# Linear attention with soft mixture of experts on one core: who copies the output banks, and a wait of three engines in front of the last branch

## Chip, core and metric

The kernel runs on one core of a Trainium2 chip. The metric is the device time of one execution in microseconds (us). Engines: PE (TensorE), DVE (VectorE), ACT (ScalarE), POOL (GpSimd) and SP (SyncE, here the queue that issues nearly all DMAs). All of a core's DMAs are carried by 16 DMA engines.

## What is computed

A gated linear attention over 4 batches x 8 heads, 768 steps, head size 48, whose result is the input x (3072 x 384) of a soft mixture of 8 experts with 4 slots each:

```python
f = 1 / (1 + np.exp(-f_logit))
for t in range(S):
    state = f[:, :, t, :, None] * state + np.einsum('bhd,bhe->bhde', k[:, :, t], v[:, :, t])
    y[:, :, t] = np.einsum('bhd,bhde->bhe', q[:, :, t], state)
x = y.transpose(0, 2, 1, 3).reshape(B * S, H * D)

logits = x @ phi                                  # 3072 x 32
d = softmax(logits, axis=0); c = softmax(logits, axis=1)
slot_input = d.T @ x                              # 32 x 384
slot_out[e] = np.maximum(slot_input[e] @ w1[e], 0) @ w2[e]
out = c @ slot_out                                # 3072 x 384
```

The output is 4.7 MB. The last line is where the change lies: 3072 x 32 by 32 x 384.

## The kernel before

Sixteen pairs of heads run through the attention in about 117 us, with loads on SP all the way. Then come the mixture's slots, the experts' first weights (`up`, L615) and second weights (`down`, L664), and the output.

The output columns are cut into three **parts** of 128 columns (`PARTS`, L32). For each part: PE multiplies the experts' second weights (`down`), DVE scales the result (`slots_out`, L675), PE sums it over the experts' rows (`slots_sum`, L678), ACT copies that to `s4` (`slots_copy`, L682), and PE forms the output rows from `s4` and the mixing weights `cT` (`combine`, L705). The rows come in six chunks of 128 for each batch: four "main" ones, and two "shared" ones whose mixing weights share a transposed tile. `combine` therefore runs twice for a part: main (four PSUM banks of 512 columns: 4 batches x 128) and shared (two banks).

**PSUM units.** PSUM is handed out by the planner as three large units of kind `a` (1024 columns, two banks) and two small ones of kind `b` (512 columns, one bank); see L232 and `unit` (L235). Before the change, main takes two `a` units and shared takes one, both of its banks in that unit. The small units carry, among others, the results of `down` (`po`) and of `slots_sum` (`so`).

**Copies and stores.** Each bank is copied to SBUF by one instruction of 512 columns (`out_copy`, L714): even banks by ACT, odd banks by DVE (L989), so each unit is read by both engines. All copies have the line of the helper, L321. The stores (`store`, L717) go out on SP: two banks together (512 KB) in parts 0 and 1, one bank (256 KB) in part 2, except that bank 4 of part 2, the first shared one, is issued on ACT's own DMA queue (L994). In part 2 the order on SP is 0, 1, 2, 3, 5.

**Order.** A planner (`Plan.run`, L119) orders everything: every operation has a cost on its engine, what it reads, writes and takes, and a due time; the planner always starts the operation that can start first. `ENDING` (L35) sets the due times of the last phase as a written sequence: `d0` a quarter of a `down` half in part 0, `s0` its sum, `c0` its two combines, and so on. Its end is `... d2 c1 s2 c2 c2`: the shared combine of part 1, the sum of part 2, and the two combines of part 2. The planned order is emitted at L1003 to L1019; `last_of` keeps the last instruction of each operation that isn't on SP, for the weights' loads that are paced by it.

**The branch.** The fast path is right only if no gate is extreme. A flag (`flag_1` to `flag_3`) says so, is loaded into a register `bad` of the engines at L1005, and after all stores have been emitted, every engine meets `tc.If(bad > 0)` (L1078). The block behind it, `general()`, is the slow path, some thousands of instructions; it is jumped over when the flag is 0, as it is for these inputs. What follows it is the end of the program: SP waits for the landings of the stores, and all engines meet in a barrier (listed under L1078 and L1133).

Of the kernel before, what the change touches and what calls it, by code (L numbers as in the profile page):

```python
# [34 lines left out]
ENDING = (  # L35
    "d0 d0 d0 d0 d0 d0 d0 d0 d1 d1 s0 d1 c0 d1 d1 d1 d1 d1 c0 s1 d2 d2 c1 d2 d2 d2 d2 d2 d2 c1 s2 c2 c2"
).split()

SWAP = NM // 2

# [32 lines left out]
class Plan:  # L73
# [22 lines left out]
    def op(self, name, engs, fn, *args, r=(), w=(), x=(), due=0.0, take=(), free=(), kb=0, home=False, ni=0):  # L96

        name, mode = name if isinstance(name, tuple) else (name, None)
        deps = set()
        for key in r:  # L100
            if key in self.writer:
                deps.add(self.writer[key])
        for key in (*w, *x):
            if key in self.writer:
                deps.add(self.writer[key])
            deps.update(self.readers.get(key, ()))
        fixed = self.fixed and "SP" not in engs
        o = Op(len(self.ops), name, engs, fn, args, due, deps, take, free, kb, home, ni, mode, fixed)
        self.ops.append(o)
        for key in w:  # L110
            self.writer[key] = o
            self.readers[key] = []
        for key in r:
            self.readers.setdefault(key, []).append(o)
        for key in (*r, *w):
            self.uses.setdefault(key, []).append(o)
        return o
# [96 lines left out]
def gla_soft_moe_kernel(ctx: ExitStack, tc: tile.TileContext, q, k, f, v, vt, phi, w1, w2, out):  # L214
# [7 lines left out]
    nc = tc.nc  # L222
# [3 lines left out]
    def P(shape, name, dt=F32):  # L226
        return pool.tile(shape, dt, tag=name, name=name)
# [5 lines left out]
    un = {}  # L233

    def unit(key):  # L235
        u = plan.unit_of[key]
        un[key] = ps.tile([128, 1024 if u[0] == "a" else 512], F32, tag=u, name=str(key[0]), bufs=1)
        return un[key]
# [9 lines left out]
    kb = [P([128, S], f"kb{i}") for i in range(N_K)]  # L248
# [71 lines left out]
    def copy(o, dst, src):  # L320
        {"ACT": nc.scalar.copy, "DVE": nc.vector.tensor_copy, "POOL": nc.gpsimd.tensor_copy}[o.eng](dst, src)  # L321
# [248 lines left out]
    def piece(part, kk):  # L570

        n = 8 * WIDE * part + WIDE * kk
        return n // PIECE, n % PIECE
# [128 lines left out]
    def staged(part, x, n=1):  # L702
        return w1b[4 + part][:, 4 * WIDE * x : 4 * WIDE * (x + n)]

    def combine(o, part, shared):  # L705

        v = [u[:, 512 * k : 512 * k + 512] for u in [unit(("pf", part, x)) for x in ((2,) if shared else (0, 1))] for k in range(2)]
        n = 128 // len(v)
        for b in range(B):
            for x, u in enumerate(v):  # L710
                gs = slice(n * x, n * x + n)
                nc.tensor.matmul(u[:, WIDE * b : WIDE * b + WIDE], cT[gs, b, shared], s4[gs, PARTS[part]], start=b == 0, stop=True, skip_group_check=True)  # L712

    def out_copy(o, part, x):  # L714
        copy(o, staged(part, x), un["pf", part, x // 2][:, 512 * (x % 2) : 512 * (x % 2) + 512])

    def store(o, part, x, n):  # L717
        at = 4 * WIDE * (6 * part + x)
# [3 lines left out]
    op = plan.op  # L722
# [181 lines left out]
    n, asked = 0, set()  # L904
# [17 lines left out]
    y = (NP - 1) * T  # L922
# [30 lines left out]
    for j in range(2):  # L953
        for hf in range(2):
            key, d = ("up", j, hf), z + 5 + 4 * j + hf
# [3 lines left out]
            key = ("turn", j, hf)  # L959
# [3 lines left out]
    def at(kind, part, n=0):  # L963

        return z + 100 + 0.1 * [x for x, name in enumerate(ENDING) if name == kind + str(part)][n]
# [5 lines left out]
    for part in range(len(PARTS)):  # L971
        key = ("po", part)
        for j in range(2):
            for k0 in range(0, 8, 2):
                ws = sorted({("w2", 2 * qq + j, piece(part, kk)[0]) for qq in range(4) for kk in (k0, k0 + 1)})
                take = [(key, "b")] if (j, k0) == (0, 0) else []
                op(("down", "strips"), {"PE": 0.47}, down, part, j, k0, k0 + 2, r=[("hT", j, k0 // 4), *ws], w=[key], due=at("d", part, 4 * j + k0 // 2), take=take, ni=32)
        op("so1", {"DVE": 0.4}, slots_out, part, r=[key, "rz", ("pin1", 0), "psi"], w=[("sob", part)], due=at("d", part, 7) + 0.05, free=[key])
        op(("so2", "square"), {"PE": 0.25}, slots_sum, part, r=[("sob", part), "same"], w=[("so", part)], due=at("s", part), take=[(("so", part), "b")], ni=4)
        op("so3", {"ACT": 0.32}, slots_copy, part, r=[("so", part)], w=[("s4", part)], due=at("s", part) + 0.05, free=[("so", part)])  # L980
        for shared in range(2):
            keys, d = [("pf", part, x) for x in ((2,) if shared else (0, 1))], at("c", part, shared)
            op(
                ("comb", "pf" + str(shared)), {"PE": 0.9}, combine, part, shared, r=[("s4", part), *(("cT", b) for b in range(B))], w=keys, due=d,
                take=[(key, "a") for key in keys], ni=16 * len(keys),
            )
            for x in range(4 * shared, 4 + 2 * shared):
                key, late = ("pf", part, x // 2), (part, x) == (2, 4)
                op("oute", [{"ACT": 0.59}, {"DVE": 0.69}][x % 2], out_copy, part, x, r=[key, ("upw", 1, 0), ("upw", 1, 1)], w=[("st", part, x)], due=d + 0.05 + 0.001 * x, free=[key])  # L989

                n = 1 if part == 2 else 2
                if (x + 1) % n == 0:
                    x0 = x + 1 - n
                    op("store", {"ACT" if late else "SP": 0.45}, store, part, x0, n, r=[("st", part, y) for y in range(x0, x0 + n)], due=d + 0.06, kb=256 * n)  # L994
    plan.fixed = False

    def emit(o):
        o.fn(o, *o.args)

    order = plan.run(dict(PE=2.3, POOL=2.3, DVE=2.0, ACT=2.1, SP=0.4))  # L1000
    written = nc.cur_bb.bb.instructions
    last_of, steps = {}, []
    for o in order:  # L1003
        if o.name == "so2" and o.args == (1,):
            bad = nc.values_load(gbad[:1, :1], min_val=0, max_val=1)  # L1005
        n0 = len(list(written))
        emit(o)
        new = list(nc.cur_bb.bb.instructions)[n0:]
        if o.name in ("lw1", "lw2"):

            before = [(d.end, n, d) for n, d in enumerate(steps) if d.end < o.begin - plan.LAT]
            if before:
                tc.add_manual_dep(
                    new[-1], last_of[max(before)[2].n], mybir.DependencyInfo(mybir.DependencyClass.Sync, mybir.DependencyReason.DATA),
                    reason="pace",
                )
        elif o.eng != "SP":
            steps.append(o)
            last_of[o.n] = new[-1].name  # L1019
    to_psi = ("gmax", "lte", "gexp", "te", "ele", "pi", "pie", "tm", "tmt", "tm2", "tmb", "twb", "twb2", "twd", "psi")  # L1020
    ending = [o for o in order if o.n >= tail_from and o.name not in (*to_psi, "flag1", "flag2", "flag3")]
    resident = [o for o in order if o.name == "lw1" and o.n < tail_from]
# [115 lines left out]
```

## Time and profile before

| | |
|---|---|
| time, median of 3 runs | 168.49 us (167.91 to 168.71) |
| the profiled execution | 168.29 us |
| its span, first to last instruction | 166.6 us |
| PE busy | 153.7 us, 92% of the span |
| DVE, ACT, POOL busy | 116.6, 94.2, 89.9 us |
| output stores | 6 of 512 KB and 5 of 256 KB on SP, 1 of 256 KB on ACT |
| issue to landing, median | 3.5 us (512 KB), 3.9 us (256 KB on SP), 4.1 us (ACT) |

The span runs from the first to the last instruction; 1.69 us of the execution lie outside it. Engines with a `q` behind the name (SPq, ACTq, PEldq) are the engines' instruction queues: DMA issues, branches and semaphore waits are listed there, and they do not count as busy time. `out<-in` names tiles: `w1a<-pf` is a copy from a combine's PSUM unit to its place in SBUF, `out_dram<-w1a` is a store. A DMA counts as landed when all of the 16 engines that carry it have reported. The DMA queues are q1 (SP's), q10 (ACT's), and q8 and q14, which load the engines' instructions.

### The profile page before, as it was taken

What the parts mean: (1) busy time and instruction counts of PE and PEld (TensorE: products, weight loads), DVE (VectorE), ACT (ScalarE), POOL (GpSimd) and SP (SyncE); (2) the same over time, 40 slices, a digit from 0 to 9 for tenths busy, and PEclk for the clock granted to TensorE, in tenths of its full rate; (3) what the DMA queues carried; (4) which work ended last, traced back from release to release, by engine and by line L of the source; (5) the groups of instructions that cost most, each with busy time, mean ns of one, the idle gap of its engine ahead of it and who ended that gap; (6) DMA issues with size and microseconds to landing.
All of it is one profiled execution on the core that took longest, in us unless ns stands there. A gap on an engine that the chain in (4) does not pass through costs nothing.

```text
span 166.6 us, 6386 instructions
## 1 busy us (share of the span) xinstructions
PE 153.7 (92%) x2724; PEld 123.3 (74%) x2724; DVE 116.6 (70%) x167; ACT 94.2 (57%) x166; POOL 89.9 (54%) x87
## 2 busy tenths in 40 slices
PE   5999999999999999999998999999899999999800
PEld 2367879889998969889896889988655449788700
DVE  4899999989979876898996989838432216043330
ACT  5899597967977949678783872631521121232310
POOL 5108969889889886897997889660000001000000
PEclk9999999999999999999999999999999999999985
DMA  5999999999999999999997559999999792055784
GB/s 134 320 407 370 390 399 398 399 398 393 395 393 397 397 397 399 396 398 398 398 377 248 182 173 293 340 363 407 398 398 389 233 360 85 6 215 211 281 295 151
DMA packets 20609, 54.05 MB, mean 325 GB/s; under 512 B 2288, under 2 KB 2912, under 8 KB 20576
## 3 DMA queue, kind: packets, MB, share of 16 engines
q1 hardware_dynamic: 20432, 53.34, 86.2%
q8 instruction: 22, 0.36, 0.9%
q10 hardware_dynamic: 144, 0.26, 0.4%
q14 instruction: 11, 0.09, 0.1%
HBM read 48.87 MB, written 4.72 MB: 322 GB/s over the span
## 4 chain that ended last, share of the span: by engine, by line
PE 67%; DVE 14%; POOL 5%; issue 4%; DMA 3%; ACT 3%; SPq 1%; POOLq 0%; ACTq 0%; DVEq 0%
PE sc L379 10%; PE y L404 9%; PE po L670 7%; PE up L625 7%; PE y L427 6%; PE kv L413 5%; PE kt L367 5%; DVE Lb L338 5%; PE xt L438 4%; PE pl L459 3%; PE pf L712 3%; DMA kb<-in_k_dram 3%; DVE scb L384 3%; POOL ce L545 2%; PE pi L502 2%
## 5 line engine op out<-in xcount | busy, mean ns | idle before, releaser
L347 POOL TENSOR_TENSOR kb<-kb,gb 112x768 f32<-112x768 f32 x15 | 27.4, 1830 | 16.3 <-ACT gb L341 12.8
L338 DVE TENSOR_TENSOR_SCAN Lb<-starts,fb 112x768 f32<-112x768 f32 (+1 forms) x17 | 35.1, 2063 | 1.6 <-ACT fb L334 1.6
L384 DVE TENSOR_TENSOR scb<-sc,mask 128x768 f32<-128x768 f32 x32 | 29.2, 950 | 4.0 <-PE sc L379 3.9
L321 POOL COPY pbx<-pb 112x240 f32<-112x240 f32 x16 | 26.6, 1663 | 4.6 <-ACT pb L344 4.6
L379 PE MATMUL sc<-qb,kb 48*128 48x128 f32 x384 | 26.5, 282 | 0.5 <-DVE kta L321 0.4
L404 PE MATMUL y<-scb,va 128*48 128x128 f32 (+1 forms) x384 | 25.9, 276 | 0.0
L379 PEld LDWEIGHTS sc<-qb,kb 48*128 48x128 f32 x384 | 22.9, 187 | 3.4 <-DVE kta L321 0.6
L321 ACT COPY yT<-y 112x768 f32<-112x768 f32 x16 | 12.8, 798 | 19.6 <-PE y L427 19.6
L347 POOL TENSOR_TENSOR qb<-qb,pb 112x768 f32<-112x768 f32 x13 | 23.7, 1827 | 0.0
L404 PEld LDWEIGHTS y<-scb,va 128*48 128x48 f32 (+1 forms) x384 | 21.9, 130 | 0.8 <-DVE scb L384 0.4
L545 POOL TENSOR_TENSOR ce<-ce,cm 128x256 f32<-128x256 f32 x4 | 4.6, 1156 | 29.7 <-DVE cm L542 29.3
L321 DVE COPY kta<-kt 128x672 f32<-128x672 f32 x14 | 11.8, 846 | 7.6 <-PE kt L367 7.6
L341 ACT ACTIVATE gb<-Lb 112x768 f32<-112x768 f32 (+1 forms) x17 | 13.7, 805 | 4.9 <-DVE Lb L338 4.9
L334 ACT ACTIVATE fb<-fb,one 112x768 f32<-112x768 f32 (+1 forms) x17 | 15.2, 897 | 0.6
L330 ACT ACTIVATE fb<-fb 112x768 f32<-112x768 f32 (+1 forms) x17 | 13.7, 805 | 2.7 <-DMA fb<-in_f_dram 2.7
L427 PE MATMUL y<-qb,sb 48*48 48x128 f32 x320 | 14.6, 285 | 0.0
L413 PE MATMUL kv<-va,kta 128*64 128x48 f32 (+1 forms) x384 | 14.4, 220 | 0.0
L413 PEld LDWEIGHTS kv<-va,kta 128*64 128x64 f32 (+1 forms) x384 | 12.4, 130 | 2.6 <-ACT kta L321 0.8
L344 ACT ACTIVATE pb<-Lb 112x768 f32<-112x768 f32 (+1 forms) x17 | 13.5, 792 | 0.0
L427 PEld LDWEIGHTS y<-qb,sb 48*48 48x48 f32 x320 | 11.1, 162 | 2.7 <-DVE sb L417 2.4
L367 PE MATMUL kt<-ident,kb 112*128 112x112 f32 x96 | 12.7, 266 | 0.2 <-POOL kb L347 0.2
L321 DVE COPY w1a<-pf 128x512 f32<-128x512 f32 x9 | 5.8, 687 | 9.5 <-ACT w1a L321 9.5
(154 smaller groups left out, 276.9 us busy)
## 6 DMA issues: line engine op xcount, KB each, us to landing
w1a<-in_w_dram SPq DMA_DIRECT2D x34, 384.0 KB, 7.6
kb<-in_k_dram SPq DMA_DIRECT2D x16, 384.0 KB, 7.4
fb<-in_f_dram SPq DMA_DIRECT2D x15, 384.0 KB, 7.3
qb<-in_q_dram SPq DMA_DIRECT2D x15, 384.0 KB, 7.3
va<-in_v_dram SPq DMA_DIRECT2D x16, 288.0 KB, 7.3
out_dram<-w1a SPq DMA_DIRECT2D x6, 512.0 KB, 3.5
scb<-in_w_dram SPq DMA_DIRECT2D x4, 384.0 KB, 6.9
out_dram<-w1a SPq DMA_DIRECT2D x5, 256.0 KB, 3.9
```

Source lines behind the costliest of these rows:

```text
L321: {"ACT": nc.scalar.copy, "DVE": nc.vector.tensor_copy, "POOL": nc.gpsimd.tensor_copy}[o.eng](dst, src)
L330: nc.scalar.activation(t, t, AF.Exp, scale=-1.0, accum_out=esum[:, n : n + 1])
L334: nc.scalar.activation(t, t, AF.Ln, bias=one[:PW])
L338: nc.vector.tensor_tensor_scan(Lb[i % N_L][:PW, cs], flat(starts)[:PW, cs], fb[i % N_F][:PW, cs], 0.0, op0=ALU.mult, op1=ALU.add)
L341: nc.scalar.activation(gb[i % N_G][:PW, cs], Lb[i % N_L][:PW, cs], AF.Exp)
L347: (nc.vector if o.eng == "DVE" else nc.gpsimd).tensor_tensor(t, t, by, op=ALU.mult)
L367: nc.tensor.transpose(u[:, C * m : C * m + PW], kb[i % N_K][:PW, C * m : C * m + C], ident[:PW, :PW])
L379: nc.tensor.matmul(u[:, 512 * r + C * m : 512 * r + C * m + C], kb[i % N_K][rs, cs], qb[i % N_Q][rs, cs], start=True, stop=True,)
L384: nc.vector.tensor_tensor(scb[i % N_SC][:, :, h], un["sc", i, h].rearrange("p (r x) -> p r x", r=2)[:, :, : 3 * C].rearrange("p r (m t) -> ...
L404: nc.tensor.matmul(u[rows(at), y_cols(m)], va[:, v0 : v0 + (D if at else 64)], scb[i % N_SC][:, r, h, m % 3], start=m % 3 == 0, stop=False ...
L413: nc.tensor.matmul(u[rows(r), :, m], ktb[i % N_KT][:, m, rows(r)], vb[i % N_V][:, m, r], start=True, stop=True)
L427: nc.tensor.matmul(u[at : at + D, y_cols(m)], sb[i % N_S][rs, :, m - 1], qb[i % N_Q][rs, C * m : C * m + C], start=False, stop=m in (2, 5) ...
```

## The change

1. **Copies.** In the main combine each unit (two banks) is read by one engine: unit 0 by ACT, unit 1 by DVE. In parts 0 and 1 that is one instruction of 1024 columns, in part 2 two of 512 each. The shared combine takes two units, one bank in each: bank 4 is copied by ACT, bank 5 by DVE. These two units are of kind `a` in parts 0 and 1, and of kind `b` in part 2.
2. **Stores.** The same pieces go out on the same queues; in part 2 the order on SP becomes 0, 2, 1, 3, 5.
3. **The wait.** After all has been emitted, and in front of the branch, PE, DVE and POOL each get a `nop` that waits until the third last store in the planner's order (`HELD = -3`) has landed. ACT and SP get none.

```diff
+HELD = -3
...
-        v = [u[:, 512 * k : 512 * k + 512] for u in [unit(("pf", part, x)) for x in ((2,) if shared else (0, 1))] for k in range(2)]
+        if shared:
+            v = [unit(("pf", part, x))[:, :512] for x in (2, 3)]
+        else:
+            v = [u[:, 512 * k : 512 * k + 512] for u in [unit(("pf", part, x)) for x in (0, 1)] for k in range(2)]
...
-    def out_copy(o, part, x):
-        copy(o, staged(part, x), un["pf", part, x // 2][:, 512 * (x % 2) : 512 * (x % 2) + 512])
+    def out_copy(o, part, x, n):
+        key, at = (("pf", part, x // 2), 512 * (x % 2)) if x < 4 else (("pf", part, x - 2), 0)
+        copy(o, staged(part, x, n), un[key][:, at : at + 512 * n])
...
-            keys, d = [("pf", part, x) for x in ((2,) if shared else (0, 1))], at("c", part, shared)
+            keys, d = [("pf", part, x) for x in ((2, 3) if shared else (0, 1))], at("c", part, shared)
+            kind = "b" if shared and part == 2 else "a"
             op(
                 ("comb", "pf" + str(shared)), {"PE": 0.9}, combine, part, shared, r=[("s4", part), *(("cT", b) for b in range(B))], w=keys, due=d,
-                take=[(key, "a") for key in keys], ni=16 * len(keys),
+                take=[(key, kind) for key in keys], ni=16 * (1 if shared else 2) * 2,
             )
-            for x in range(4 * shared, 4 + 2 * shared):
-                key, late = ("pf", part, x // 2), (part, x) == (2, 4)
-                op("oute", [{"ACT": 0.59}, {"DVE": 0.69}][x % 2], out_copy, part, x, r=[key, ("upw", 1, 0), ("upw", 1, 1)], w=[("st", part, x)], due=d + 0.05 + 0.001 * x, free=[key])
-
-                n = 1 if part == 2 else 2
-                if (x + 1) % n == 0:
-                    x0 = x + 1 - n
-                    op("store", {"ACT" if late else "SP": 0.45}, store, part, x0, n, r=[("st", part, y) for y in range(x0, x0 + n)], due=d + 0.06, kb=256 * n)
+
+            for key, eng in zip(keys, ("ACT", "DVE")):
+                x0, n = (2 + key[2], 1) if shared else (2 * key[2], 2)
+                step = 1 if part == 2 else n
+                for x in range(x0, x0 + n, step):
+                    op(
+                        "oute", {eng: {"ACT": 0.14, "DVE": 0.07}[eng] + {"ACT": 0.45, "DVE": 0.61}[eng] * step}, out_copy, part, x, step,
+                        r=[key, ("upw", 1, 0), ("upw", 1, 1)], w=[("st", part, y) for y in range(x, x + step)], due=d + 0.05 + 0.001 * x, free=[key],
+                    )
+
+            n = 1 if part == 2 else 2
+            for x in (4, 5)[::n] if shared else (0, 2, 1, 3) if n == 1 else (0, 2):
+                late = (part, x) == (2, 4)
+                op("store", {"ACT" if late else "SP": 0.45}, store, part, x, n, r=[("st", part, y) for y in range(x, x + n)], due=d + 0.06, kb=256 * n)
...
+        elif o.name == "store":
+            last_of[o.n] = new[-1].name
         elif o.eng != "SP":
...
+    stored = last_of[[o for o in order if o.name == "store"][HELD].n]
+    for eng in (nc.tensor, nc.vector, nc.gpsimd):
+        eng.nop()
+        tc.add_manual_dep(
+            list(written)[-1], stored, mybir.DependencyInfo(mybir.DependencyClass.Sync, mybir.DependencyReason.DATA), reason="leave",
+        )
```

## The prediction

> **What bounds the kernel now.** The change touches only what follows the last down products, so I first read the chain that ended last for its final pieces, then the windows of the last 10 us, then the rows of the stores and of the branch. The page's span, PE's last products from the timeline (start, duration; both combines of part 2), and the end of the chain (start, duration):
>
> ```profile
> span 166.6 us, 6386 instructions
> ...
> 156.15 2.27 PE L712 MATMUL pf<-pin,cT 32*128 32x128 f32 x48 [0.43 <-ACT pin L321]
> ...
> 157.36 0.59 ACT w1a L321
> ...
> 157.98 0.52 DVE w1a L321
> ...
> 158.59 0.59 DVE w1a L321
> ...
> 159.18 0.68 DVE w1a L321
> ```
>
> Computation ends at 159.18 + 0.68 = 159.86; the span ends at 166.6. So 6.7 us are stores and closing. The columns of the next view are busy time by engine, then granted clock, share of the 16 DMA engines, GB/s:
>
> ```profile
> 158.80:160.20 1.40, 0.00 (x0) 0.00 (x0) 1.06 (x2) 0.25 (x1) 0.00 (x0) 1.00 0.99 360
> 160.40:161.10 0.70, 0.00 (x0) 0.00 (x0) 0.00 (x0) 0.00 (x0) 0.00 (x0) 1.00 0.15 47
> 161.20:164.00 2.80, 0.00 (x0) 0.00 (x0) 0.00 (x0) 0.00 (x0) 0.00 (x0) 0.50 1.01 372
> 164.20:164.50 0.30, 0.00 (x0) 0.00 (x0) 0.00 (x0) 0.00 (x0) 0.00 (x0) 0.50 0.12 48
> 164.70:166.60 1.90, 0.00 (x0) 0.00 (x0) 0.00 (x0) 0.00 (x0) 0.00 (x0) 0.50 0.00 0
> ```
>
> The stores move at 360 to 372 GB/s, with a hole from about 160.4 to 161.1 (share 0.15), and after 164.1 two engines of sixteen (0.12) work on alone until 164.7.  Why the hole? The issues on the two queues (start, duration):
>
> ```profile
> 157.97 0.33 SPq L719 DMA_DIRECT2D out_dram<-w1a  x1
> 158.70 0.33 SPq L719 DMA_DIRECT2D out_dram<-w1a  x1
> 159.08 1.61 ACTq L719 DMA_DIRECT2D out_dram<-w1a  x1
> 159.12 1.70 SPq L719 DMA_DIRECT2D out_dram<-w1a  x1
> 161.39 0.69 SPq L719 DMA_DIRECT2D out_dram<-w1a  x1
> DMA to landing us min/median/max: 3.7/3.7/3.7
> ```
>
> A store takes 0.33 us to issue, but those of 159.1 take 1.6 and 1.7. The last one (its landing is the last row) goes out at 161.39 and lands at 165.1, though its data was ready at 159.86. Beside the stall lie the branch and its code pages:
>
> ```profile
> L1078 POOLq COMPARE_BRANCH  x1: 65/65/65, 141.4 to 141.4; - x1
> L1078 PEldq COMPARE_BRANCH  x1: 491/491/491, 157.3 to 157.3; - x1
> L1078 PEldq EVENT_SEMAPHORE  x1: 51/51/51, 158.5 to 158.5; - x1
> L1078 DVEq COMPARE_BRANCH  x1: 84/84/84, 159.1 to 159.1; - x1
> L1078 ACTq COMPARE_BRANCH  x1: 68/68/68, 160.7 to 160.7; - x1
> L1078 SPq COMPARE_BRANCH  x1: 70/70/70, 162.1 to 162.1; - x1
> L1133 SPq DRAIN  x3: 7/7/7, 165.8 to 166.1; - x3
> L1133 PEldq DRAIN  x2: 8/8/8, 158.6 to 166.1; - x2
> ```
>
> The queue table, for the whole run, for 158.9 to 160.6 and for 159.2 to 159.35, shows instruction loads (packets, MB, share of 16 engines), pages of 0.36/22 MB = 16 KB on q8 and 0.09/11 MB = 8 KB on q14:
>
> ```profile
> q8 instruction: 22, 0.36, 0.9%
> q14 instruction: 11, 0.09, 0.1%
> ...
> q14 instruction: 2, 0.02, 2.3%
> ...
> q8 instruction: 1, 0.02, 49.5%
> ```
>
> A 16 KB page starts between 159.2 and 159.35 and holds one engine for 0.495 x 16 x 0.15 = 1.19 us, to about 160.45; the stalled issues end at 160.69 and 160.82, right behind. PE passed the branch at 157.3; the page follows its jump. The two smaller ones last 0.023 x 16 x 1.7 / 2 = 0.31 us each; one follows DVE's jump. The stall has a precedent in the load phase: an issue of 0.94 us in a window (100.5 to 102.5) with one such page. A counterexample is the second pair (window 129.9 to 131):
>
> ```profile
> 101.87 0.94 SPq L568 DMA_DIRECT2D va<-in_w_dram  x1
> q8 instruction: 1, 0.02, 5.9%
> ...
> 130.33 0.33 SPq L568 DMA_DIRECT2D w1a<-in_w_dram  x1
> q8 instruction: 1, 0.02, 5.3%
> ```
>
> So a page can stall an issue, but does not always. So the end is set by late issue, one late DMA engine, landing, then closing.
>
> **Copies by one engine.** The waits, the copies' durations, the widest other copies, and DVE's part 1 from the timeline:
>
> ```profile
> DVE w1a L321 <- ACT w1a L321: 9.5, 5, 3.7
> L321 ACT COPY w1a<-pf x9: 586/586/591, 145.5 to 158.5; 128x512 f32<-128x512 f32 x9
> L321 DVE COPY w1a<-pf x9: 680/691/692, 146.1 to 159.2; 128x512 f32<-128x512 f32 x9
> L321 ACT COPY yT<-y 112x768 f32<-112x768 f32 x16 | 12.8, 798 | 19.6 <-PE y L427 19.6
> L321 DVE COPY kta<-kt 128x672 f32<-128x672 f32 x14 | 11.8, 846 | 7.6 <-PE kt L367 7.6
> ...
> 152.10 1.29 DVE L321 COPY w1a<-pf 128x512 f32<-128x512 f32 x2 [1.83 <-ACT w1a L321]
> 154.28 0.35 DVE L676 TENSOR_SCALAR pin<-po,zr 128x128 f32<-128x128 f32 x1 [0.89 <-PE po L670]
> ```
>
> DVE's copy of a unit's second bank starts 0.02 to 0.03 us behind ACT's end of the first: they are ordered, and DVE starts a whole ACT copy (0.59) late. After the change ACT and DVE start together. Parts 0 and 1: one 1024 wide copy each. ACT: 586 + 512 x (798 - 586)/256 = 1.01 us; DVE: 691 + 512 x (846 - 691)/160 = 1.19 us. From the end of the products the two stores can go at 1.03 and 1.22 us instead of 0.59 + 0.02 + 0.69 = 1.30 and 1.90. Four wide copies replace eight; DVE has time for them before its next scaling (it sits idle 0.89 us ahead of the one at 154.28, and will be done 0.7 earlier). Part 2 keeps its six copies of 512: ACT ends as now (158.46 + 0.59 = 159.05), DVE runs from 157.36 at a pitch of 0.60 (158.59 to 159.18): 157.36, 157.96, then the shared bank when the products end, 156.15 + 2.27 = 158.42, plus 0.04 and 0.69: **159.2 instead of 159.86**. The shared products of part 2 move to the two small units, free when the scaling (DVE) and s4 copy (ACT) have read them; the main products wait for that s4 copy already (0.43 in the row), so: nothing. In parts 0 and 1 they take two of three large units; those are free more than 0.3 us before PE comes, by the copy lengths above. PE's instructions stay the same in number: zero there.
>
> The copies alone are worth little: before the change the data was waiting for SP's queue, not the reverse. They matter once the stall is gone.
>
> **Stores.** Order on SP: banks 0, 2, 1, 3, 5; bank 4 on ACT. Data at 157.95, 158.05, 158.43, 158.65, 159.2 and 159.05. SP's pitch is 159.12 - 158.70 = 0.42, so five issues start at 157.97, 158.39, 158.81, 159.23, 159.65, and the last ends at 159.98, not at 161.39 + 0.69 = 162.08. The shared store of part 1 can go 0.6 earlier, as its DVE copy does. I count it as zero: the engines run full from 158.80 on in any case, and what it clears before then is at most the backlog of a late engine, inside the bounds below.
>
> **The wait in front of the branch.** PE, DVE and POOL get one empty instruction each that waits for the landing of the third last store in the planner's order. By its costs that is bank 4 on ACT (its start comes out 0.005 us ahead of bank 3's, so it may be bank 3). Nothing is queued behind these instructions but the branch and the closing; no copy, product or store. What leaves the store phase is PE's 1.19 us page and DVE's 0.31; POOL's jump was at 141.4 and cost nobody anything. ACT and SP aren't held: their pages (0.31 each) stay, and come earlier, as their branches do (160.7 and 162.1 now, near 159.5 and 160.1 then).
>
> **Sum.** Data starts about 0.45 us after an issue ends (stalled ones end 160.69 and 160.82, flow is full from 161.2): first store ends issue at 158.30, data from 158.8. Six stores of 262 KB are 1.573 MB, at 372 GB/s 4.23 us: 163.0. From the end of data to landing 165.1 - 164.7 = 0.4: 163.4. Test on the present run: four stores from 161.2 take 2.82, to 164.0, plus 0.65 for the late engines, plus 0.4: 165.1, as measured. For the late engine after the change the bounds are 0 (no page where the bytes are) and 1.2 (PE's page, or three small ones with their aftermath, meet the last stores again). I take 0.5, nearest to the 0.65 of the row, because two small pages stay: last landing **163.9**, 1.2 earlier. Closing from landing to span's end stays 166.6 - 165.1 = 1.5, so the span is 165.4. The held engines hide behind it: bank 4 issues at 159.08, shares the engines with SP's queue and lands near 162; PE's branch (0.49), jump (157.77 to 158.47) and drain need 1.35 us, and SP drains 0.7 us after the last landing, so PE is late only if the held landing comes less than 0.65 us before the last. Expected distance: 1.2 or more.
>
> The profiled execution took 168.29 us, 1.69 beside its span, so 167.1; the median of the runs shown is 168.49, 0.2 above that. I forecast **167.2**.
>
> The Trainium skill (DMA: Bandwidth & Descriptors, section "Why a DMA increments its semaphore by 16 and not by 1") says that each DMA engine reports on its own and only the full count means landed. The trace agrees: 0.12 of the engines work on after the rest. If the mean engine decided, the sum would be 163.4 and 166.6 instead.
>
> **Rivals.**
> - *Most comes back* (0.22): the stall is that of a full queue and not of the page, or released pages meet the last two stores. For it: bank 4 may land as early as 161.5, then PE's page comes 2 us later (157.3 to 159.26 now), and the pages of ACT and SP sit in a fuller stream; at 130.33 a page stalled nothing. Against: stalls end with the page. The last landing is then 163.4 + 1.2 = 164.6: 167.8.
> - *Jump waits for its page* (0.06): held engines reach the closing only after a load. PE would need 0.49 + 1.5 + 1.19 after 162, so 165.2, and the closing of 0.75 behind a drain ends at 166.0 instead of 165.4: 167.7. Against it: PE's first instruction after the jump ran at 158.5, before the page began. The Trainium skill (Runtime: NRT & Kernel Launch, section "Instruction fetch mechanics") says that a taken branch to a page outside the window must wait for its load; by that rule this case holds, while the trace disagrees, and its small pages are 8 KB where the section has 16.
> - *The held engines become the end* (0.08, slower): the third last store lands with the last, as when ACT's queue or one DMA engine is behind. Decides from 0.65 us before the last landing. If the stall also stays (landing 165.1), PE drains at 166.45, closing 0.75 ends at 167.2, and its page (from 1.5 after the branch, 1.19 long) may run on for 1.1 us: 168.9 to 170.0; I name 169.4.
> - *All gained* (0.12): no late engine, landing 163.2 or before: 166.4.
> - Forecast: 0.52.
>
> **How the numbers follow.** A measurement of this kernel can tell some 0.5%, 0.84 us, from no change. Faster by more (below 167.65): forecast and all gained, 0.64. Within: the first two rivals and the part of the slower one under 169.3, here 0.06 + 0.22 + 0.01 = 0.29. Slower: 0.07. The range goes from 166.3 (all gained) to 168.3 (most comes back, plus 0.5 for a worse late engine); the slower case and the far tails stay outside.
>
> **What would show it.** Right: no store issue over 1 us after 157.9; no hole in the DMA share between 159 and 163; q8's last page behind 162.5; last landing near 163.9; DVE's pf copies no longer waiting for ACT's. Wrong: a 1.6 us issue with no page beside it (full queue); PE's drain later than SP's (held engines are the end); a page inside the last two stores; or a last landing near 165 with all issues on time, meaning that the bytes of one DMA engine alone set the end.

## The result, and the profile after

| | before | after |
|---|---|---|
| median of 20 runs each | 168.13 us (167.78 to 169.04) | 167.36 us (166.76 to 169.6) |
| ratio, 95% interval | | 0.9949 (0.993 to 0.9968) |
| the same kernel on another chip (run e3) | 168.55 us, 23 runs | 166.98 us, 6 runs: 0.9912 (0.988 to 0.9944) |
| profiled execution, its span | 168.29, 166.6 us | 167.51, 165.8 us |

The kernel is faster by 0.5 to 0.9%. The forecast of 167.2 us was 0.16 us low, inside its range. The run of 169.6 us was in a slower state that the chip sometimes takes; the ratios leave such runs out.

The two profiles can't be compared by their clocks alone. PE's first score products, in the timelines of before, after and e3 (start, duration), show why:

```profile
8.02 0.94 PE L379 MATMUL sc<-qb,kb 48*128 48x128 f32 x12
```

```profile
8.32 0.94 PE L381 MATMUL sc<-qb,kb 48*128 48x128 f32 x12 [0.51 <-DVE qb L349]
```

```profile
7.75 0.94 PE L381 MATMUL sc<-qb,kb 48*128 48x128 f32 x12
```

The first profile after the change lost 0.3 us behind its first loads and carried that to the end; e3, the same kernel, gained 0.3 there. So all that follows is measured from **ACT's first copy of part 2's output**, where the changed stretch begins: 157.36 before, 157.70 after. From there to the end of the span, the "end stretch", is 166.56 - 157.36 = 9.20 us before and 165.78 - 157.70 = 8.08 after (8.09 in e3). The change is worth 1.12 us there.

The end of the chain and DVE's copies in the timeline, after the change:

```profile
156.49 1.24 PE pf L717 x32
...
158.37 1.28 DVE w1a L323 x2
```

```profile
151.90 1.23 DVE L323 COPY w1a<-pf 128x1024 f32<-128x1024 f32 x1 [1.64 <-PE pf L717]
154.63 0.35 DVE L678 TENSOR_SCALAR pin<-po,zr 128x128 f32<-128x128 f32 x1 [1.51 <-PE po L672]
157.76 1.89 DVE L323 COPY w1a<-pf 128x512 f32<-128x512 f32 x3 [1.34 <-PE pf L717]
```

DVE now waits for PE, not for ACT (one copy of part 0, at 149.57, waits for a store to land). The last copy ends at 158.37 + 1.28 = 159.65, 1.95 behind the first copy's start instead of 2.50. The issues of part 2's stores, in order (timeline; the last two rows are the last store's, from the store tile's view):

```profile
158.31 0.33 SPq L725 DMA_DIRECT2D out_dram<-w1a  x1
158.74 0.38 SPq L725 DMA_DIRECT2D out_dram<-w1a  x1
159.21 0.39 SPq L725 DMA_DIRECT2D out_dram<-w1a  x1
159.40 0.38 ACTq L725 DMA_DIRECT2D out_dram<-w1a  x1
159.70 0.41 SPq L725 DMA_DIRECT2D out_dram<-w1a  x1
160.20 1.15 SPq L725 DMA_DIRECT2D out_dram<-w1a  x1
...
L725 SPq DMA_DIRECT2D out_dram<-w1a x1: 1152/1152/1152, 160.2 to 160.2; - x1
DMA to landing us min/median/max: 4.1/4.1/4.1
```

The stalls of 1.6 and 1.7 us are gone; only the last issue takes 1.15, with no store queued behind it. The windows (last two columns: share of the DMA engines, GB/s) have no hole among part 2's stores any more:

```profile
159.20:163.20 4.00, 0.00 (x0) 0.00 (x0) 0.45 (x1) 0.17 (x1) 0.00 (x0) 1.00 1.03 381
163.40:163.80 0.40, 0.00 (x0) 0.00 (x0) 0.00 (x0) 0.00 (x0) 0.00 (x0) 0.95 0.13 51
```

381 GB/s without a break, then two engines of sixteen (0.13) that run on alone. A pause has come in front of part 2's first bytes instead (share 0.07, 21 GB/s from 158.6 to 159.0), a time that the stores of part 1 filled before the change. The branch rows:

```profile
L1100 ACTq COMPARE_BRANCH  x1: 68/68/68, 160.1 to 160.1; - x1
L1100 SPq COMPARE_BRANCH  x1: 70/70/70, 161.4 to 161.4; - x1
L1100 DVEq COMPARE_BRANCH  x1: 84/84/84, 162.8 to 162.8; - x1
L1100 PEldq COMPARE_BRANCH  x1: 491/491/491, 162.8 to 162.8; - x1
L1100 PEldq EVENT_SEMAPHORE  x1: 51/51/51, 163.3 to 163.3; - x1
...
L1100 ACTq EVENT_SEMAPHORE  x1: 17/17/17, 163.7 to 163.7; - x1
```

PE, DVE and POOL go at 162.78, when ACT's store of bank 4 has landed. ACT, which isn't held, takes 3.6 us from its branch to its next instruction (160.1 to 163.7).

### The profile page after: what moved, and what is told of

It is laid out like the page before. It is cut to its first block, busy times and chain, and to the rows that moved or that the text cites. A ratio compares the mean times of both kernels' runs of the same rounds, so it can differ in the third digit from the quotient of the medians.

```text
span 165.8 us, 6378 instructions
## 1 busy us (share of the span) xinstructions
PE 153.4 (93%) x2724; PEld 123.3 (74%) x2724; DVE 116.4 (70%) x165; ACT 94.0 (57%) x164; POOL 90.0 (54%) x87
## 4 chain that ended last, share of the span: by engine, by line
PE 67%; DVE 14%; issue 5%; POOL 4%; DMA 3%; ACT 2%; SPq 1%; POOLq 0%; ACTq 0%; DVEq 0%
PE sc L381 10%; PE y L406 9%; PE po L672 7%; PE up L627 7%; PE y L429 6%; PE kv L415 5%; PE kt L369 5%; DVE Lb L340 5%; PE xt L440 4%; PE pl L461 3%; PE pf L717 3%; DMA qb<-in_q_dram 3%; DVE scb L386 3%; POOL ce L547 2%; PE pi L504 2%
## 5 line engine op out<-in xcount | busy, mean ns | idle before, releaser
L419 DVE TENSOR_TENSOR_SCAN sb<-kv,pbx 112x288 f32<-112x288 f32 x16 | 12.0, 747 | 0.0
```

## The experiments

Each store is carried by 16 DMA engines, and each of them reports its share. In the table, "typical" is the ninth report of the sixteen, "last" the sixteenth, each the latest over part 2's six stores; "late" is their difference. Times are in us from ACT's first copy of part 2. "Longest issue" is that of part 2's stores. Two quantities tell the theories apart: a stalled issue moves the typical engine's end, a page in the way of one DMA engine moves only the last report.

| run | ratio (95%) | end stretch | typical | last | late | longest issue |
|---|---|---|---|---|---|---|
| before | 1 | 9.20 | 7.06 | 7.75 | 0.69 | 1.70 |
| after | 0.9949 (0.993 to 0.9968) | 8.08 | 6.03 | 6.63 | 0.60 | 1.15 |
| e1 copies only | 0.9956 (0.9931 to 0.998) | 8.72 | 6.57 | 7.27 | 0.69 | 1.79 |
| e2 wait only | 0.9978 (0.9955 to 1.0) | 9.07 | 6.10 | 7.43 | 1.33 | 1.52 |
| e3 after again | 0.9912 (0.988 to 0.9944) | 8.09 | 6.02 | 6.63 | 0.61 | 1.14 |
| e4 only PE waits | 0.9918 (0.9886 to 0.9949) | 8.24 | 6.04 | 6.78 | 0.75 | 1.12 |
| e5 ACT waits too | 0.9932 (0.9915 to 0.9948) | 8.07 | 6.02 | 6.61 | 0.59 | 1.16 |
| e6 for the last store | 1.0002 (0.9979 to 1.0026) | 9.06 | 6.72 | 7.59 | 0.88 | 2.02 |
| e7 for the seventh last store | 1.0014 (0.9997 to 1.0031) | 9.45 | 6.00 | 7.99 | 1.99 | 1.15 |
| e8 wait only, all on SP | 0.9966 (0.995 to 0.9982) | 8.81 | 6.04 | 7.35 | 1.31 | 1.00 |
| e9 ACT's page moved | 0.9932 (0.9908 to 0.9956) | 8.10 | 6.03 | 6.64 | 0.61 | 1.15 |
| e10 ACT's page early, ACT waits too | 0.9929 (0.9905 to 0.9952) | 8.08 | 6.03 | 6.63 | 0.59 | 1.15 |
| e11 as e10, SP waits too | 0.9884 (0.9857 to 0.991) | 7.53 | 5.98 | 6.08 | 0.10 | 1.14 |
| e12 SP waits too | 0.9932 (0.9907 to 0.9956) | 8.09 | 5.97 | 6.63 | 0.67 | 1.15 |

e1 to e4 ran on one chip, e5 to e8 on a second, e9 to e12 on a third, each beside the kernel before. The stretch is from one profile, and repeats to 0.01 us in e3. Each interval holds the ratio that the stretch alone would give (for the change, 1.12 us of 168.1 is 0.9933), but the intervals are too wide to part neighbours such as e3 and e4: such differences rest on one profile each.

**e1: the copies and the store order alone.**

```diff
-    stored = last_of[[o for o in order if o.name == "store"][HELD].n]
-    for eng in (nc.tensor, nc.vector, nc.gpsimd):
...
```

> The new copies and store order without the wait in front of the branch. The end stretch is the time from the first copy of part 2 to the end of the span: 9.2 us before the change, 8.1 after it. Theory A (PE's code page behind its jump stalls the issues and makes one DMA engine late): the page is back among the stores of part 2 and an issue of over 1 us beside it; end stretch 8.9 to 9.3, ratio 0.998 to 1.000. Theory B (the earlier copies brought the gain): end stretch 8.1 to 8.5, ratio 0.995 to 0.997. Theory C (the long issues come from a full queue or from two queues issuing together): long issues as in A, but not tied to the page in time.

SP's long issue, the queue table for 158.6 to 160, and two windows:

```profile
158.54 1.79 SPq L725 DMA_DIRECT2D out_dram<-w1a  x1
...
q8 instruction: 1, 0.02, 5.5%
```

```profile
158.90:160.20 1.30, 0.00 (x0) 0.00 (x0) 0.55 (x1) 0.28 (x1) 0.00 (x0) 1.00 0.65 235
161.00:163.60 2.60, 0.00 (x0) 0.00 (x0) 0.00 (x0) 0.00 (x0) 0.00 (x0) 0.50 1.03 381
```

The page is back, starting 158.71 and taking 0.055 x 16 x 1.4 = 1.23 us, and it lies inside the long issue of 158.54; ACT's store at 159.21 took only 0.38. So the stall came with the page, and not from two queues issuing together. The window of 158.9 to 160.2 shows the price: 235 GB/s, where 161 to 163.6 has 381. Theory A is right on the mechanism, but not on the size: the stretch of 8.72 lies between its 8.9 to 9.3 and theory B's 8.1 to 8.5, and the ratio lies in B's range. The copies and their store order alone bring 0.48 of the 1.12 (by the medians on this chip, 0.83 of 1.57 us).

**e2 and e8: the wait alone.** Both have the first two lines put in; the last line, which gives SP all stores, is e8's only.

```diff
+    stored = last_of[[o for o in order if o.name == "store"][HELD].n]
+    for eng in (nc.tensor, nc.vector, nc.gpsimd):
...
-                    op("store", {"ACT" if late else "SP": 0.45}, store, part, x0, n, r=[("st", part, y) for y in range(x0, x0 + n)], due=d + 0.06, kb=256 * n)
+                    op("store", {"SP": 0.45}, store, part, x0, n, r=[("st", part, y) for y in range(x0, x0 + n)], due=d + 0.06, kb=256 * n)
```

> The copies and the store order of before, with the wait of PE, DVE and POOL. Theory A: no 16 KB page and no issue over 1 us among the first five stores of part 2; the stores are limited by their bytes, so the late copies cost 0 to 0.4; end stretch 8.1 to 8.5, ratio 0.995 to 0.998. Theory B: end stretch 8.8 to 9.2, ratio 0.999 to 1.001. Theory C: issues of over 1 us at the store that goes out together with ACT's, with no page beside them.

> The copies of before with the wait, and all stores on SP (none on ACT). In the run with the wait alone ACT's store took 1.5 us to issue with no 16 KB page beside it, and landed last. Theory D (ACT's issue lost against SP's, 0.04 us apart, and that took the wait's gain): no issue over 1 us except perhaps the last, end stretch 8.1 to 8.5, ratio 0.993 to 0.997. If the late copies are what the wait alone lacks: 8.7 to 9.1, ratio near 0.998.

The profile of e2: ACT's store in the timeline and its landing, PE's branch, and windows:

```profile
159.04 1.52 ACTq L720 DMA_DIRECT2D out_dram<-w1a  x1
...
DMA to landing us min/median/max: 5.7/5.7/5.7
...
L1087 PEldq COMPARE_BRANCH  x1: 481/481/481, 164.8 to 164.8; - x1
...
158.80:163.20 4.40, 0.00 (x0) 0.00 (x0) 1.02 (x2) 0.21 (x1) 0.00 (x0) 1.00 0.97 359
163.50:164.20 0.70, 0.00 (x0) 0.00 (x0) 0.00 (x0) 0.00 (x0) 0.00 (x0) 0.50 0.05 12
```

No 16 KB page lies among the stores, and the hole is gone (0.97 from 158.8 on; the typical engine ends at 6.10, 0.96 earlier than before). But nearly all of it is lost again at the end, and the stretch of 9.07 misses theory A's 8.1 to 8.5: one engine of sixteen (0.05) runs on alone for 0.7 us and more, and ACT's store, issued 0.04 us ahead of one of SP's, took 1.52 us to issue and landed last of all. It is the store for which the engines wait, so PE's branch came at 164.8, and the closing, from the last landing to the end of the span, was 1.64 instead of 1.46. By the trace's rows, 0.13 of these 0.18 us are SP's: it looks at the stores' semaphores one after the other, and two stood behind that of ACT's store. Only 0.05 is a wait for a held engine (DVE), the prediction's slower rival. e8 takes ACT's queue away, and the held store is then the fourth of part 2: no long issue but the last, closing 1.46 again. Still the late engine cost 1.31, and the stretch was 8.81, not the 8.1 to 8.5 of theory D (the ratio, 0.9966, lies in its range). So ACT's slow issue was 0.26 of the lost gain, the late engine most of the rest; the late copies cost the typical engine nothing (6.04).

That ACT lost a race against SP's issue, as theory D has it, isn't shown. A rival fits the traces better: ACT waited for its own code. An 8 KB page that seems to be ACT's next one (e9 below moves such a page by adding ACT copies) takes from 1.72 to 2.03 in e2, and ACT's issue, begun at 1.72, ends 1.22 behind it. In after, e1, e3 to e8 and e12 ACT's first instruction behind its branch comes 1.22 to 1.28 behind the end of such a page, wherever the page lies. Before the change the same page lies at the same place and ACT's stalled issue ends 1.31 behind it, so that stall too need not be PE's page. No run parts the two.

**e3 and e4: the change again, and with PE alone waiting.**

```diff
-    for eng in (nc.tensor, nc.vector, nc.gpsimd):
+    for eng in (nc.tensor,):
```

> The changed kernel once more, on the same chip as the parts: ratio 0.993 to 0.997, end stretch 8.0 to 8.2 by all theories. If its first score starts at 8.0 instead of 8.3 us, the 0.37 us that its first profile lost at the start was chance and the span is about 165.4.

> The change with only PE waiting; DVE and POOL go through the branch at once. Theory A with the 16 KB page as the main cause: end stretch 8.1 to 8.4, ratio 0.994 to 0.997. If the small 8 KB pages of DVE cost as much: 8.5 or more, ratio above 0.997.

Holding PE gives 8.24, the three together 8.08: PE's page is worth 8.72 - 8.24 = 0.48 with the new copies, DVE's 0.16. POOL's page came at 142.8 in e4, long before the stores.

**e7: the wait ends earlier.**

```diff
-HELD = -3
+HELD = -7
```

> The change with the wait for the seventh last store, the shared one of part 1, which lands some 2.2 us behind the first copy of part 2: the pages of PE, DVE and POOL then start some 1.2 to 2 us later, when nearly all stores have been issued but not landed. Theory A, late engine: one engine's landings are 0.6 to 1.3 us behind the others', end stretch 8.5 to 9.0, ratio 0.997 to 0.999. If a page hurts only by stalling issues: 8.0 to 8.2.

PE's branch, the last store's issue and landing, the windows, and the pages between 161 and 163.7:

```profile
L1100 PEldq COMPARE_BRANCH  x1: 491/491/491, 159.2 to 159.2; - x1
...
L725 SPq DMA_DIRECT2D out_dram<-w1a x1: 1152/1152/1152, 159.4 to 159.4; - x1
DMA to landing us min/median/max: 5.5/5.5/5.5
...
158.40:162.40 4.00, 0.00 (x0) 0.00 (x0) 0.47 (x1) 0.20 (x1) 0.00 (x0) 0.67 1.03 374
162.70:163.40 0.70, 0.00 (x0) 0.00 (x0) 0.00 (x0) 0.00 (x0) 0.00 (x0) 0.50 0.18 47
163.40:164.40 1.00, 0.00 (x0) 0.00 (x0) 0.00 (x0) 0.00 (x0) 0.00 (x0) 0.50 0.13 39
...
q14 instruction: 5, 0.04, 3.9%
q8 instruction: 1, 0.02, 2.3%
```

This separates the two costs. No issue is stalled that anything waits for, and the typical engine ends at 6.00, as after the change. But all six pages meet the last stores, two or three engines (0.18, then 0.13) run on until 164.4, and the last report is 1.99 us late. The stretch is 9.45, longer than before the change and than the 8.5 to 9.0 expected. **A page need not stall an issue to cost its time: it is enough that it lies in front of one engine's last bytes.** It also shows that the wait is of use only if it ends late enough.

**e6: the wait for the last store.**

```diff
-HELD = -3
+HELD = -1
```

> The change with the wait for the last store in the planner's order instead of the third last. Rival of the prediction (held engines become the end): the closing, last landing to end of span, grows from 1.45 to 2.1 or more, end stretch 8.6 or more. By the trace of the changed kernel (PE drains 0.70 us behind its branch's start, SP 0.70 us behind the last landing): closing 1.4 to 1.6, end stretch 8.0 to 8.2, the same as with the third last.

```profile
L1100 PEldq COMPARE_BRANCH  x1: 492/492/492, 156.9 to 156.9; - x1
...
L1155 PEldq COMPARE_BRANCH  x1: 195/195/195, 164.6 to 164.6; - x1
...
L725 SPq DMA_DIRECT2D out_dram<-w1a x1: 2016/2016/2016, 158.0 to 158.0; - x1
```

The question wasn't answered: no row of the empty instruction stands in the traces, its wait sits on the next branch, and here that was one behind the jump (L1155) instead of L1100. PE passed L1100 at 156.9 as without a wait, the page came and one issue took 2.02 us. As it stands the run is a second e1, and again shows page and stall together.

**e5, e9, e10, e12: which small pages are left.** The late 0.60 of the changed kernel comes with two 8 KB pages, 4.48 and 5.80 us behind the first copy. e5 makes ACT wait too (the first new line), e12 makes SP wait too (the second, in its place):

```diff
-    for eng in (nc.tensor, nc.vector, nc.gpsimd):
+    for eng in (nc.tensor, nc.vector, nc.gpsimd, nc.scalar):
+    for eng in (nc.tensor, nc.vector, nc.gpsimd, nc.sync):
```

e9 adds five one-column copies to ACT near 137 us; e10 adds 8 in each of three of ACT's idle stretches (130 to 138 us) and makes ACT wait (the diff is e9's; in e10 and e11 the counts are 0, 8, 8, 8):

```diff
     def up_copy(o, j, hf):
         u = un["up", j, hf][:, :512]
+        for _ in range((0, 0, 0, 5)[2 * j + hf]):
+            nc.scalar.copy(pad, one)
```

> The change with ACT waiting in front of the branch too, for the same store. End stretch 8.1 us in the changed kernel. Theory A extended (each code page among the stores makes one DMA engine late, the 8 KB ones too): ACT's page leaves the store phase, the last landing of all comes within 0.3 us of the typical engine's (now 0.6), end stretch 7.8 to 8.0, ratio 0.001 to 0.002 under the changed kernel's. If only the 16 KB page counts: 8.0 to 8.2 and no difference.

> The changed kernel with five one-column ACT copies more, in ACT's idle time near 137 us, into a scratch column that nothing reads. In the kernels with the old copies (ACT has five instructions more there) an 8 KB page comes 1.7 us behind the first copy of part 2, and ACT's jump takes 0.5 us; with the new copies it comes 4.5 us behind, and ACT's jump takes 3.6 us. Theory E (the page is ACT's next one, and its place follows from the number of ACT's instructions; the old copies' page makes an engine late from the first store on): page back at 1.2 to 1.8, ACT's jump 0.5, end stretch 8.3 to 8.7, ratio 0.996 to 0.999. Rival (the place of the page has nothing to do with ACT's count): end stretch 8.0 to 8.2, page at 4.5.

> The changed kernel with SP waiting too, ACT as in the change. Theory A extended: the page at 5.8 us behind the first copy moves behind the stores, the one at 4.5 stays; end stretch 7.8 to 8.0. If SP's jump comes too late: closing 1.7 or more.

> The changed kernel with 24 such copies (8 in each of three idle stretches of ACT, 130 to 138 us), so that ACT's page is loaded there, and ACT waiting with the others. Theory E: no page at 4.5, the last landing of all within 0.3 to 0.5 us of the typical engine's, end stretch 7.8 to 8.0, ratio 0.001 to 0.002 under the changed kernel's. Rival (that page costs nothing): 8.0 to 8.2.

All four ended at 8.07 to 8.10, like the changed kernel, so the expected tenths of e5, e10 and e12 did not come, nor the loss of e9. But the pages moved. In e5 they stayed at 4.47 and 5.80, so ACT's branch doesn't set the first. In e9 one came at -0.51 and none at 4.48, and ACT's jump took 0.5 us instead of 3.6:

```profile
L1102 ACTq COMPARE_BRANCH  x1: 68/68/68, 159.7 to 159.7; - x1
L1102 ACTq EVENT_SEMAPHORE  x1: 17/17/17, 160.2 to 160.2; - x1
```

With the 24 copies of e10 it came at -24.5. So that page is ACT's next one in order, it comes the earlier the more instructions ACT has run, and ACT's jump waits for it. (The size was wrong: it came 2 us earlier than expected, in front of the stores, and ACT's page behind the jump, now at 4.97, and SP's at 5.80 took its place.) In e12 the page of 5.80 moved to 6.27 and later, so it is SP's. In e10 only SP's, at 5.79, is left of the two. The two pages make the end late in different ways. The queue rows of e10 for 162.70 to 163.00 and of e12 for 162.90 to 163.15:

```profile
q14 instruction: 3, 0.02, 25.8%
...
q1 hardware_dynamic: 3, 0.01, 6.3%
```

In e12 one engine (0.063 x 16 = 1) still moves store bytes, behind ACT's page. In e10 pages alone are moved: by the packets' own times all store bytes are down at 5.80, just as SP's page starts, and yet one report comes at 6.63, 0.83 behind, where the others come 0.34 to 0.41 behind their bytes. So a page that starts right behind an engine's last bytes seems to hold its report too; how, no run shows.

**e11: both.** The copies of e10, and five engines waiting:

```diff
-    for eng in (nc.tensor, nc.vector, nc.gpsimd):
+    for eng in (nc.tensor, nc.vector, nc.gpsimd, nc.scalar, nc.sync):
```

> As the run with 24 copies, with SP waiting too: all five engines pass the branch when ACT's store has landed. Theory A extended: no code page among the last stores, the last landing within 0.3 us of the typical engine's (6.0 us behind the first copy), closing 1.46 as before since SP's jump (0.5) ends ahead of the last landing: end stretch 7.5 to 7.8, ratio 0.988 to 0.993. Rival (SP's branch behind the wait makes the closing late): closing 1.7 or more, end stretch 8.0 or more.

Branch and waits of e11, its last two stores, windows, and the pages from 162.8 to 163.5:

```profile
L1102 SPq EVENT_SEMAPHORE  x8: 17/17/17, 162.4 to 163.3; - x8
L1102 SPq COMPARE_BRANCH  x1: 70/70/70, 161.8 to 161.8; - x1
L1102 ACTq COMPARE_BRANCH  x1: 68/68/68, 161.9 to 161.9; - x1
...
L727 SPq DMA_DIRECT2D out_dram<-w1a x2: 400/771/1142, 159.1 to 159.6; - x2
DMA to landing us min/median/max: 3.4/3.5/3.6
...
158.60:162.60 4.00, 0.00 (x0) 0.00 (x0) 0.45 (x1) 0.18 (x1) 0.00 (x0) 0.84 1.03 383
...
q14 instruction: 4, 0.03, 17.6%
q8 instruction: 1, 0.02, 11.8%
```

Each alone gave nothing, both together 0.55 us: all sixteen engines report within 0.10 of the typical one, and the last store lands 3.6 us behind its issue instead of 4.1. With both pages two engines report late (6.41 and 6.63 in the last store after the change), with either page one (6.63 in e10 and e12), and the end waits for the latest report, so either page alone holds the same end. In e11 the first page starts at 5.82, 0.12 behind the last store bytes; in e10 it was 5.79. The median is 166.28 us beside 168.08 before, 0.9884 (0.9857 to 0.991), and beside 166.97 to 167.11 of e9, e10 and e12 on the same chip, which have the changed kernel's end stretch. Holding SP costs nothing here, since its jump (0.5 us behind 161.85) is done 0.8 us ahead of the last landing.

## Why the prediction was right, point by point

- **The end was stores, not computation, and a code page behind PE's jump stalled them: right, for SP's issue.** With the page (before, e1, e6) an issue takes 1.7 to 2.0 us and the typical engine ends at 6.6 to 7.1; without it (after, e3 to e5, e7 to e12) it ends at 5.97 to 6.04, in e2 at 6.10. SP's stalled issue ends 0.37 to 0.40 behind the end of PE's page in all three. ACT's, which the prediction put down to the same page, took 1.52 in e2 without it.
- **The sum: right nearly term by term.** Typical landing 163.4 on the clock of before, 6.04 behind the first copy; measured 6.03. Late engine 0.5; measured 0.60. Closing 1.5; measured 1.46. Sum 8.04; measured 8.08. That the time came within 0.16 is in part luck. It stood on the median of three runs (168.49), which twenty runs put at 168.13; the gain forecast on it was 1.29, the medians differ by 0.77. And its last step adds 0.1 of the 0.2 by which it puts the median above the profile; with all of it the forecast is 167.3. In the end stretch, which leaves out what varies ahead of part 2, the working holds: a gain of 1.16 forecast, 1.12 measured.
- **DVE's copies by row: right.** 1024 columns forecast at 1.19 us on DVE and 1.01 on ACT; measured 1.22 and 1.01. Last copy 0.66 earlier forecast, 0.55 measured: DVE's first started 0.06 behind ACT's, and its third had to wait for the second (by the forecast's own pitch 157.96 + 0.60 = 158.56, not 158.46).
- **"The copies alone are worth little": wrong.** They bring 0.48 alone, the wait 0.13 alone, both 1.12. The step that failed took the stall as a fixed block in front of the last issues. In e1 the page starts 1.20 behind the first copy instead of 1.90 and the stall ends at 2.82 instead of 3.46, so three of SP's stores follow it from an earlier point. That the stores of part 1 left earlier, and with them the backlog of the engine that carries the page, would explain the earlier page; this was only argued. The new copies and order also move ACT's 8 KB page and ACT's issue away from SP's, and no run parts these from the copies' speed.
- **The wait's cost: right, with a wrong number.** The held store was ACT's, as worked out, and landed at 5.05, not near 4.6. PE's chain from branch to drain is 0.70 us, not 1.35: in the profile before, PE's next instruction behind the jump stood waiting for its products, which I had read as the jump. The two errors work against each other.
- **"No store issue over 1 us": wrong, without effect.** The last issue takes 1.15 us with no page of PE near it (1.00 to 1.16 in e3 to e5, e7 to e12). When it starts, the typical engine has five stores ahead of it (four in e8). In e1 and e6 it had three, and the issue took 0.43 and 0.41; in e2 SP's last issue took 0.40 while ACT's was still stuck. That fits a limit on what is in flight, but no run tested it, and before the change the last issue took 0.69 with three ahead.
- **Rival "most comes back": it is what e7 and, in part, e2 show.** The released pages then meet the last stores. In the change they start 6.2 us or more behind the first copy, when the typical engine is done. The margin is small: 2.8 us earlier is worse than no wait.
- **Rival "jump waits for its page": wrong for PE, DVE and POOL** (0.5 to 0.6 us, branch to next instruction), **right for ACT**, which the prediction had not named: 3.6 us after the change. It is hidden, since SP looks at ACT's semaphore only at 164.9. The Trainium skill (Runtime: NRT & Kernel Launch, section "Instruction fetch mechanics") has the rule that a taken branch outside the fetched pages waits for its load. By that rule a held engine could become the end; the trace agrees only in part. ACT's jump does wait for a page, and e9's five copies make the wait vanish. But in e5 that page came at 4.47, ahead of ACT's branch at 5.06, so it isn't shown to be the page of the jump's target.
- **Slower rival: seen only in e2,** where the held store was the last to land, and there as 0.05 of the 0.18 us by which the closing grew.

What stays open: what stalled ACT's issue in e2, and why the late engine is 1.3 us late with the wait alone, but 0.6 after the change. In e2 and e8 an 8 KB page comes 1.7 us behind the first copy, and two engines report 0.5 late from the first store on; e9 was to bring that page back and put it elsewhere, so the link isn't shown.

## What to carry to other kernels

A store is done when its slowest DMA engine is done, and instruction pages travel on the same engines: when a kernel ends in stores, look for the pages that a jump or a page boundary sends among them, and let the engines that have finished wait in front of the jump until the stores are nearly down. Time that wait by the trace, since too early is worse than none, and an empty instruction may hand its wait to one behind the jump. When removing one cause changes nothing, remove it together with the other suspects before calling it harmless: two late engines hide each other.

## What the runs showed of the hardware

- An 8 KB instruction page among or right behind the last stores took 0.31 us by its own row, but one of the sixteen reports came about 0.6 us late (e10, e12: 0.59 and 0.67 with one such page left; 0.10 with none in e11).
- A 16 KB page of PE, 1.19 to 1.47 us by its rows, beside a store's issue on SP made that issue take 1.7 to 2.0 us instead of 0.33 to 0.38 (before, e1, e6), and the other DMA engines ran dry meanwhile (share 0.15 from 160.4 to 161.1 before, 0.65 from 158.9 to 160.2 in e1). In the load phase before the change a page at 130.33 stalled no issue.
- From an engine's branch to its page took 2.1 us where stores filled the DMA engines (after: SP, 161.4 to 163.5; but 1.3 for PE in e1, 157.4 to 158.7) and 1.1 where they had none (before: POOL, 141.4 to 142.55).
- The place of a page can decide how long a jump takes: 0.5 or 3.6 us on ACT for the same branch, five copies apart (e9 and after). Where ACT waited for such a page, it went on 1.22 to 1.28 us behind the page's end, in nine runs.
